# Turning the third pair's second tile behind the first six products of the next tile, with another order of the blocks

## The chip, the cores and the metric

The kernel runs on one core of a Trainium2 chip. The metric is the device time of one execution in microseconds (us), taken as the median of three executions. The core has a matrix engine (PE, with a weight load, PEld, beside it), a vector engine (DVE), a scalar engine (ACT), a general engine (POOL) and a queue for transfers (SP). Each engine takes its instructions in the order in which the program gives them; semaphores hold an instruction back until what it needs is there.

## What is computed

```python
def _A_ref(x, dft_seq_re, dft_seq_im, dft_hid_re, dft_hid_im):
    a = jnp.einsum("bsd,ed->bse", x, dft_hid_re)
    b = jnp.einsum("bsd,ed->bse", x, dft_hid_im)
    return jnp.einsum("ts,bse->bte", dft_seq_re, a) - jnp.einsum("ts,bse->bte", dft_seq_im, b)

def _B_ref(x, w1, b1, w2, b2):
    y = _layernorm(x, axis=-1)
    h = _gelu(jnp.einsum("bsd,df->bsf", y, w1) + b1)
    return jnp.einsum("bsf,fd->bsd", h, w2) + b2

x = A_x
x = x + _A_ref(_layernorm(x, axis=-1), ...)
x = x + _B_ref(_layernorm(x, axis=-1), B_w1, B_b1, B_w2, B_b2)
x = x + _A_ref(_layernorm(x, axis=-1), ...)
x = x + _B_ref(_layernorm(x, axis=-1), B_w1, B_b1, B_w2, B_b2)
```

There are 2048 tokens of 576 values, an inner width of 4608, and two layers of one Fourier mixing and one perceptron each, all in float32. The perceptron's weights are drawn 200 times larger than usual.

## The kernel before

A float32 number is cut into a **high part**, which is the number rounded to a short float format (ACT writes it, in a copy with the output type `F32R`), and a **low part**, which is the rest (DVE subtracts). A product of two numbers then takes three passes on PE: high by high, high by low, low by high (`PASSES`). The large products go by Strassen's scheme with seven block products, numbered 1 to 7, in place of eight. The sums of blocks that this needs are made by DVE and POOL.

A layer is a `Sequence` (the product along the tokens) and then, for each half of 1024 tokens, `hidden` (the product along the 576 values) followed by `mlp` (the perceptron). `hidden` runs four times in the program, and it is what the change touches. It takes eight tiles of 128 tokens, n = 0 to 7. For each it makes 54 products: nine slices k of the inner dimension, three passes, two halves of 288 columns. At the end of a tile DVE adds the result to the tile's x (line 199, shape 128x576), `norms(n)` takes its mean and variance on DVE (L227 to L235), POOL raises the variance to the power -1/2 (L233), and one tile later, ahead of its products, ACT makes the shift (L239) and the normalized tile (L259).

Two tiles that follow each other are a **pair** j. The even tile gives the normalized blocks b11 and b21, the odd one b12 and b22 (each 128 tokens by 288 values; they lie at the places 2, 3 and 0, 1 of `t8[j]`). `mlp` wants them with the tokens along the columns, in seven forms: three of the blocks themselves, and four sums of blocks. For the pairs 0, 1 and 2 this goes as follows.

- `rests(j)`: a block has 288 values, two times 128 and a rest of 32. ACT copies the rests of the four blocks into a small tile `es`, in two groups of 128 columns. In each group one block is the **host**, with three copies of its rest, and another is the **guest**, with one copy in the last 32 columns (L994, L996).
- `turn_blocks(j)`: PE transposes the four blocks (L1010, eight transposes) and the two groups of `es` (L1013, two). ACT copies the result out of PSUM: the eight in one instruction (L1014), then the hosts' rests (L1016) and three copies of the guests' rests (L1020).
- `turn_sums(j)` and `parts`: ACT writes the high parts of the plain blocks (L1028; 128x768 for two blocks, 128x384 for one, 128x1536 for the four sums), DVE their low parts (L202 with a first row of 32 partitions), and DVE makes the four sums of blocks (L202, 128x384, `A<-A`).
- `turn_parts(j)`: the high and low parts of the four sums.

The fourth pair is handled otherwise. Its sums are made by DVE before it is turned (four L202 of 128x288, after a normalization that DVE itself makes on line 978), and `turn_y` transposes seven blocks one after the other (L1059, 14 transposes; its rests on L1069), ACT and DVE cutting them straight from PSUM (`split`, L205 and L202). `mlp` is a generator; its first seven steps are 7 products of 256 columns each, on the first two pairs, and they stand between the last tile's products and `turn_y`: five of them ahead of L1059, the other two behind it.

The order is written out by hand in the loop over n:

```python
            if n in (3, 5):
                turn_parts((n - 3) // 2)
            if n >= 2 and n % 2 == 0:
                turn_blocks(n // 2 - 1)
            if n == NP - 2:
                turn_sums(2)
```

So the pair 2 (the tiles 4 and 5) is turned after the products of tile 6. The normalization of tile 6 stands at the head of the round of tile 7, behind it. The table `RIGHT_T` says at which place of `y` each of the seven forms lies.

Of the kernel before, what the change touches and what calls it, by code (L numbers as in the profile page):

```python
# [10 lines left out]
AF = mybir.ActivationFunctionType  # L11
# [4 lines left out]
P = 128  # L16
NT = S // P
DH = D // 2
NP = NT // 2
# [20 lines left out]

RIGHT = {1: 0, 3: 1, 2: 2, 5: 3, 6: 4, 7: 5, 4: 6}
LEFT = {1: 0, 2: 1, 4: 2, 5: 3, 6: 4, 7: 5, 3: 6}
RIGHT_T = {3: 0, 2: 1, 1: 2, 5: 3, 7: 4, 6: 5, 4: 6}

OUTER = ((1, 6, 5, 3), (7, 4, 2))
LAST = (1, 2, 6, 5, 7, 3, 4)
# [115 lines left out]
def spectral_mixer(ctx: ExitStack, tc: tile.TileContext, x, dh, c0, cs, w1, b1, w2, b2, out):  # L162
# [8 lines left out]
    nc = tc.nc  # L171
# [18 lines left out]
    ident = const.tile([P, P], F32, name="ident")  # L190
# [7 lines left out]
    def add(engine, dst, a, b, op=OP.add):  # L198
        engine.tensor_tensor(dst, a, b, op=op)  # L199

    def sub(engine, dst, a, b):
        engine.tensor_tensor(dst, a, b, op=OP.subtract)  # L202

    def split(hi, lo, src):
        nc.scalar.activation(hi, src, AF.Copy)  # L205
        sub(nc.vector, lo, src, hi.bitcast(F32))
# [4 lines left out]
    def mm(o, a, b, start, stop):  # L211
        nc.tensor.matmul(o, a, b, start=start, stop=stop, skip_group_check=True)  # L212
# [122 lines left out]
    class Sequence:  # L335
# [405 lines left out]
        def post(self, t, i):  # L741
# [26 lines left out]
            if i == 6 and self.late or t == NT - 1 and i == 4:  # L768
# [3 lines left out]
                self.late = None  # L772

        def run(self, hidden):
            for p in range(NP):
                while self.ready <= p:
# [43 lines left out]
    class Hidden:  # L820
# [106 lines left out]
        def turn(self, n, place=None):  # L927
            if n >= NP:
                return
            v = self.uv[n](2 * D)  # L930
            v = (v.bitcast(F32) if self.half else v).rearrange("p (q k t) -> p k q t", q=4, t=32)
            self.ut[n] = place or R.place(UT_AT[self.half][n % 2], 2 * KH * P)
            o = self.ut[n](2, KH, 4, 32)
            split(o[:, 0], o[:, 1], v)
            yield
            self.uvs.give(self.uv.pop(n))

    def drain(*gens):
        gens = list(gens)
        while gens:  # L940
            for g in list(gens):
                if next(g, "end") == "end":
                    gens.remove(g)

    def hidden(h, mlp):
# [4 lines left out]
        def space():  # L950
            return pp[ring.pop(0)] if ring else h.space()
# [6 lines left out]
        y = Y(7, 5, TC)  # L958
# [31 lines left out]
        def rests(j):  # L990
            v = t8[j](8, DH)
            if j < 3:
                e = es(7 * 3 * 32)[:, :2 * P].rearrange("p (n c i) -> p n c i", n=2, c=4)
                nc.scalar.activation(e[:, :, 0:3], v[:, 1:4:2, None, 2 * P:].to_broadcast([P, 2, 3, 32]), AF.Copy)  # L994
                for n, k in enumerate((2, 0)):
                    nc.scalar.activation(e[:, n, 3], v[:, k, 2 * P:], AF.Copy)  # L996
                return
            e = es(7, 3, 32)
            nc.scalar.activation(e[:, :, 1].bitcast(F32R), v[:, 1:8, 2 * P:], AF.Copy)
            nc.gpsimd.tensor_copy(e[:, :, 0], v[:, 1:8, 2 * P:])  # L1000
            sub(nc.gpsimd, e[:, :, 2], v[:, 1:8, 2 * P:], e[:, :, 1])

        def turn_blocks(j):


            v, x = t8[j](8, DH), t8[j](8 * DH)[:, 6 * P:].rearrange("p (b k t) -> p b k t", b=4, k=3)
            a, b = space(), space()
            for n, e in enumerate((2, 0, 1, 3)):
                for k in range(2):
                    nc.tensor.transpose(a[:, n // 2, (n % 2 * 2 + k) * P:(n % 2 * 2 + k + 1) * P],  # L1010
                                        v[:, e, k * P:(k + 1) * P], ident)
            for n in range(2):
                nc.tensor.transpose(b[:, 0, n * P:(n + 1) * P], es(7 * 3 * 32)[:, n * P:(n + 1) * P], ident)  # L1013
            nc.scalar.activation(x[:, :, 0:2], a.rearrange("p a (b k t) -> p (a b) k t", k=2, t=P), AF.Copy)  # L1014
            o = b[:, 0, :2 * P].rearrange("p (b t) -> p b t", t=P)
            nc.scalar.activation(x[:96, 2:4, 2], o[:96], AF.Copy)  # L1016
            if j == 2:
                parts(j, slice(2, 4), slice(0, 2), low=False)
            for c in range(3):
                nc.scalar.activation(x[32 * c:32 * c + 32, 0:2, 2], o[96:], AF.Copy)  # L1020

        def parts(j, block, i, high=True, low=True, engine=nc.vector):


            x = t8[j](8 * DH)[:, 6 * P:].rearrange("p (b k t) -> p b k t", b=4, k=3)[:, block]
            at = slice(j * P, (j + 1) * P)
            if high:
                nc.scalar.activation(y[:, i, 0:3, at], x, AF.Copy)  # L1028
            if low:
                sub(engine, y[64:96, i, 2, at], x[64:96, :, 2], y[64:96, i, 2, at].bitcast(F32))  # L1030
                sub(nc.vector, y[:, i, 3:5, at], x[:, :, 0:2], y[:, i, 0:2, at].bitcast(F32))

        def turn_sums(j):
            x = t8[j](8 * DH)[:, 6 * P:].rearrange("p (b k) -> p b k", b=4)
            b11, b12, b22, b21 = (x[:, k] for k in range(4))
            parts(j, slice(2, 4), slice(0, 2), high=j < 2)
            parts(j, slice(0, 1), slice(2, 3))
            g = nc.vector
            sub(g, b11, b12, b11)
            sub(g, b12, b22, b12)  # L1040
            sub(g, b22, b22, b11)
            sub(g, b21, b21, b22)

        def turn_parts(j):
            parts(j, slice(0, 4), slice(3, 7))
            t8s.give(t8.pop(j))

        def turn_y(j):
            v = t8[j](8, DH)
            at = slice(j * P, (j + 1) * P)  # L1050
            blocks = (1, 3, 2, 4, 5, 6, 7)
            for m, i0 in enumerate((2, 4, 0, 6)):
                if m % 2 == 0:
                    o = space()
                ob = o[:, m % 2]
                ni = min(2, 7 - i0)
                for i in range(ni):
                    for k in range(2):
                        nc.tensor.transpose(ob[:, (2 * i + k) * P:(2 * i + k + 1) * P],  # L1059
                                            v[:, blocks[i0 + i], k * P:(k + 1) * P], ident)  # L1060
                ov = ob[:, :2 * ni * P].rearrange("p (i k t) -> p i k t", k=2, t=P)
                split(y[:, i0:i0 + ni, 0:2, at], y[:, i0:i0 + ni, 3:5, at], ov)
                yield
            o = space()
            for i0 in (0, 4):
                ov = o[:, i0 // 4].rearrange("p (i t) -> p i t", t=P)
                ni = min(4, 7 - i0)
                for i in range(ni):
                    nc.tensor.transpose(ov[:96, i], es(7, 96)[:, blocks[i0 + i] - 1], ident)  # L1069
                nc.scalar.activation(y[:96, i0:i0 + ni, 2, at], ov[:96, :ni], AF.Copy)  # L1070
                yield
            t8s.give(t8.pop(j))

        ln = iter(())
        for n in range(NP):
            h.load(n + 2)
            for k in (n,) if n < NP - 1 else (n, n + 1):
                h.keep_d(k)
            if n:
                drain(turn(n + 1))  # L1080
                next(ln)
            if n >= 2 and n % 2 == 0:
                rests(n // 2 - 1)
            if n == NP - 3:
                next(mlp)
            o = space()
            if n == NP - 1:

                h.uvs.close()
                next(mlp)  # L1090
                o, ring = pp[3], [2, 3] * 3
            u = h.ut.pop(n)
            for k in range(KH):
                if n == 0 and k == KH // 2:
                    drain(turn(1))
                if n in (3, 5) and k == 2:
                    turn_sums((n - 3) // 2)
                if k == 4:
                    next(ln, None)
                for m, (a, b) in enumerate(PASSES):  # L1100
                    for e in range(2):
                        mm(o[:, e, :DH], u(2, KH, P)[:, a, k], h.dd[k][b](2, DH)[:, e],
                           k == 0 and m == 0, k == KH - 1 and m == 2)
            u.free()
            clock[0] += 1
            tile_x = xv[:, :, order[n]]
            add(nc.vector, tile_x, o[:, :, :DH], tile_x)
            ln = norms(n)
            next(ln)
            if n in (3, 5):  # L1110
                turn_parts((n - 3) // 2)
            if n >= 2 and n % 2 == 0:
                turn_blocks(n // 2 - 1)
            if n == NP - 2:
                turn_sums(2)


        for _ in range(2):
# [27 lines left out]
    def mlp(hid, store, first, ends, before, after):  # L1146
# [102 lines left out]
        def inner(q, part=None):  # L1249
# [12 lines left out]
            for i in ORDER:  # L1262
                if part != 0:
                    load_w(2, 1)
                w = got1[q, i](5, P)
                yi = y[:, RIGHT_T[i]][:, :, at]
                o = b[BANK[i]][:, at]
# [267 lines left out]
```

## Time and profile before

| | |
|---|---|
| median of three executions | 2617.44 us |
| the three | 2616.97, 2617.44 and 3634.14 us |
| the profiled execution | 2617.61 us |
| its span, first to last instruction | 2615.8 us |
| PE busy | 2609.1 us of the span, 17228 products and transposes |
| DVE, ACT, POOL busy | 1826.2, 1133.5, 788.8 us |
| granted PE clock | full speed in all 40 slices |

Between the profiled execution's time and its span lie 1.8 us around the first and the last instruction. A row of the timeline has its start, its length, the engine, the line, the operation, what is written and read, the shape, and how many instructions were merged into it; idle time ahead of it and what ended that stand in brackets. Of instructions that overlap, a row's length runs to the end of the last one.

### The profile page before, as it was taken

What the parts mean: (1) busy time and instruction counts of PE and PEld (TensorE: products, weight loads), DVE (VectorE), ACT (ScalarE), POOL (GpSimd) and SP (SyncE); (2) the same over time, 40 slices, a digit from 0 to 9 for tenths busy, and PEclk for the clock granted to TensorE, in tenths of its full rate; (3) what the DMA queues carried; (4) which work ended last, traced back from release to release, by engine and by line L of the source; (5) the groups of instructions that cost most, each with busy time, mean ns of one, the idle gap of its engine ahead of it and who ended that gap; (6) DMA issues with size and microseconds to landing.
All of it is one profiled execution on the core that took longest, in us unless ns stands there. A gap on an engine that the chain in (4) does not pass through costs nothing.

```text
span 2615.8 us, 44812 instructions
## 1 busy us (share of the span) xinstructions
PE 2609.1 (100%) x17228; PEld 2463.2 (94%) x17228; DVE 1826.2 (70%) x2581; ACT 1133.5 (43%) x1881; POOL 788.8 (30%) x639
## 2 busy tenths in 40 slices
PE   9999999999999999999999999999999999999999
PEld 9999999899999989999999999999999999899998
DVE  9999987878777765556687667576555557555555
ACT  7555556555553543333354433353333325433332
POOL 6334333545443332122340000133222232322222
PEclk9999999999999999999999999999999999999999
DMA  6666676778788566666544333756666685666664
GB/s 226 216 248 245 240 252 217 282 273 300 280 288 309 164 209 193 195 220 203 181 178 138 117 121 119 210 166 191 196 196 196 195 268 169 199 195 194 194 195 154
DMA packets 223237, 544.89 MB, mean 208 GB/s; under 512 B 23712, under 2 KB 74912, under 8 KB 222880
## 3 DMA queue, kind: packets, MB, share of 16 engines
q1 hardware_dynamic: 210352, 513.58, 60.9%
q10 hardware_dynamic: 12672, 28.45, 2.8%
q8 instruction: 136, 2.23, 0.3%
q14 instruction: 77, 0.63, 0.1%
HBM read 429.87 MB, written 114.72 MB: 208 GB/s over the span
## 4 chain that ended last, share of the span: by engine, by line
PE 97%; ACT 1%; DVE 1%; issue 0%; DMA 0%; POOL 0%; ACTq 0%; DVEq 0%; POOLq 0%
PE bank L212 96%; PE bank L1010 0%; DVE R L202 0%; PE bank L1461 0%; DMA w_parts<-R 0%; ACT A L259 0%; DVE A L202 0%; PE bank L1059 0%; ACT R L205 0%; ACT A L1020 0%; DVE A L199 0%; POOL moments L233 0%; DVE moments L227 0%; PE bank L1069 0%; ACT R L1028 0%
## 5 line engine op out<-in xcount | busy, mean ns | idle before, releaser
L212 PE MATMUL bank<-R 128*128 128x288 f32 (+2 forms) x16972 | 2582.3, 314 | 0.6 <-ACT A L759 0.2
L212 PEld LDWEIGHTS bank<-R 128*128 128x128 f32 x16972 | 2434.0, 188 | 144.6 <-DVE A L199 1.1
L199 DVE TENSOR_TENSOR A<-bank,A 128x576 f32<-128x576 f32 (+3 forms) x812 | 568.1, 707 | 513.5 <-PE bank L212 457.7
L202 POOL TENSOR_TENSOR R<-A,R 128x512 fp32r<-128x512 f32 (+1 forms) x292 | 379.5, 1308 | 907.7 <-ACT R L1324 565.6
L202 DVE TENSOR_TENSOR R<-A,R 128x1024 fp32r<-128x1024 f32 (+10 forms) x534 | 530.7, 1017 | 56.1 <-ACT R L714 26.0
L1324 ACT ACTIVATE R<-A 128x512 fp32r<-128x512 f32 x288 | 177.4, 630 | 354.8 <-DVE A L202 221.2
L199 POOL TENSOR_TENSOR A<-A 128x576 f32<-128x576 f32 (+2 forms) x102 | 151.4, 1493 | 532.5 <-ACT A L759 359.1
L1259 ACT ACTIVATE bank<-bank,b1t 128x512 f32<-128x512 f32 (+1 forms) x224 | 144.9, 647 | 351.1 <-DVE bank L199 232.6
L199 DVE TENSOR_TENSOR bank<-bank,A 128x512 f32<-128x512 f32 (+1 forms) x228 | 152.3, 670 | 143.3 <-PE bank L212 142.7
L714 ACT ACTIVATE R<-A 128x1024 fp32r<-128x1024 f32 x196 | 204.2, 1053 | 107.0 <-PE bank L212 62.1
L202 POOL TENSOR_TENSOR A<-A 128x288 f32<-128x288 f32 (+3 forms) x152 | 192.1, 1268 | 187.2 <-DVE R L202 112.6
L202 DVE TENSOR_TENSOR A<-A 128x1024 f32<-128x1024 f32 (+3 forms) x166 | 159.0, 962 | 5.3
L202 DVE TENSOR_TENSOR R<-bank,R 128x512 fp32r<-128x512 f32 x232 | 156.2, 676 | 5.5 <-ACT R L1324 5.0
L1324 ACT ACTIVATE R<-bank 128x512 fp32r<-128x512 f32 x216 | 121.4, 595 | 34.4 <-PE bank L212 34.4
L202 DVE TENSOR_TENSOR A<-bank,A 128x512 f32<-128x512 f32 x144 | 98.1, 681 | 0.3
L1286 ACT ACTIVATE A<-bank 128x512 f32<-128x512 f32 (+1 forms) x76 | 43.8, 577 | 114.4 <-PE bank L212 114.3
L285 ACT ACTIVATE R<-A 128x256 fp32r<-128x256 f32 x126 | 51.9, 412 | 85.1 <-DMA w_parts<-R 56.5
L1259 ACT ACTIVATE A<-bank,b1t 128x512 f32<-128x512 f32 (+1 forms) x76 | 50.6, 665 | 63.8 <-DVE bank L199 63.8
L233 POOL TENSOR_TENSOR moments<-moments,power 128x1 f32<-128x1 f32 x32 | 25.6, 799 | 142.8 <-DVE moments L235 114.3
L286 ACT ACTIVATE R<-A,power,middle 128x128 fp32r<-128x128 f32 x126 | 60.6, 481 | 0.0
L259 ACT ACTIVATE A<-A,moments 128x576 f32<-128x576 f32 x58 | 49.3, 867 | 21.6 <-DMA A<-x_mid 11.2
L1194 ACT ACTIVATE R<-A 128x576 fp32r<-128x576 f32 x63 | 42.2, 676 | 16.6 <-DVE A L202 7.1
(74 smaller groups left out, 617.2 us busy)
## 6 DMA issues: line engine op xcount, KB each, us to landing
R<-w_parts SPq DMA_DIRECT2D x504, 320.0 KB, 3.4
R<-w_parts SPq DMA_DIRECT2D x189, 576.0 KB, 3.7
A<-in_cs SPq DMA_DIRECT2D x112, 512.0 KB, 4.5
w_parts<-R SPq DMA_DIRECT2D x63, 576.0 KB, 6.0
w_parts<-R ACTq DMA_DIRECT2D x76, 320.0 KB, 4.9
uv_mid<-A SPq DMA_DIRECT2D x28, 576.0 KB, 5.7
w_parts<-R SPq DMA_DIRECT2D x50, 320.0 KB, 4.8
A<-in_w SPq DMA_DIRECT2D x72, 192.0 KB, 5.4
```

Source lines behind the costliest of these rows:

```text
L199: engine.tensor_tensor(dst, a, b, op=op)
L202: engine.tensor_tensor(dst, a, b, op=OP.subtract)
L212: nc.tensor.matmul(o, a, b, start=start, stop=stop, skip_group_check=True)
L233: nc.gpsimd.tensor_tensor(mv[:, 3:4], mv[:, 2:3], power[:, 0:1], op=OP.pow)
L259: nc.scalar.activation(dst, src, AF.Identity, bias=mv[:, 4:5], scale=mv[:, 3:4])
L285: nc.scalar.activation(t[:, 1:4:2], src[:, 0:3:2], AF.Copy)
L286: nc.scalar.activation(t[:, 2], src[:, 1], AF.Identity, bias=power[:, 2:3], scale=middle)
L714: nc.scalar.activation(self.cells[t, i](2, NP, P)[:, 0], self.source(t, i), AF.Copy)
L1194: nc.scalar.activation(got2[g, i](2, 2, DH)[:, :, 0], src, AF.Copy)
L1259: nc.scalar.activation(dst, src, AF.Gelu_apprx_tanh, bias=bias(f))
L1286: nc.scalar.activation(up, o, AF.Copy)
L1324: nc.scalar.activation(H[q, k](2, TC)[:, 0], src, AF.Copy)
```

## The change

The second tile of the pair 2 is turned apart from the first. `turn_blocks` becomes a generator with a `yield` after the four transposes of the even tile; what is left (the four of the odd tile, the two groups of rests, and all copies) and `turn_sums(2)` run inside tile 7, behind its slice k = 0, which is six products. The hosts of the rests are b22 and b11, where they were b22 and b21, and the guests b12 and b21, where they were b11 and b12; by their places in `t8[j]` the copies of the rests are two instructions, not three. In `turn_sums` three of the four sums stand ahead of the low part of the guest block b21. `RIGHT_T` and the slices in `turn_y` follow the new places in `y`; the order in which `turn_y` transposes its blocks stays.

```diff
-RIGHT_T = {3: 0, 2: 1, 1: 2, 5: 3, 7: 4, 6: 5, 4: 6}
+RIGHT_T = {3: 0, 2: 1, 1: 2, 6: 3, 7: 4, 5: 5, 4: 6}
...
-                nc.scalar.activation(e[:, :, 0:3], v[:, 1:4:2, None, 2 * P:].to_broadcast([P, 2, 3, 32]), AF.Copy)
-                for n, k in enumerate((2, 0)):
-                    nc.scalar.activation(e[:, n, 3], v[:, k, 2 * P:], AF.Copy)
+                nc.scalar.activation(e[:, :, 0:3], v[:, 1:3, None, 2 * P:].to_broadcast([P, 2, 3, 32]), AF.Copy)
+                nc.scalar.activation(e[:, :, 3], v[:, 0:4:3, 2 * P:], AF.Copy)
...
-            for n, e in enumerate((2, 0, 1, 3)):
+            for n, e in ((2, 2), (3, 3), (1, 0), (0, 1)):
+                if n == 1:
+                    yield
...
-            nc.scalar.activation(x[:96, 2:4, 2], o[:96], AF.Copy)
+            nc.scalar.activation(x[:96, 0:3:2, 2], o[:96], AF.Copy)
             if j == 2:
-                parts(j, slice(2, 4), slice(0, 2), low=False)
+                parts(j, slice(0, 3, 2), slice(0, 3, 2), low=False)
             for c in range(3):
-                nc.scalar.activation(x[32 * c:32 * c + 32, 0:2, 2], o[96:], AF.Copy)
+                nc.scalar.activation(x[32 * c:32 * c + 32, 1:4:2, 2], o[96:], AF.Copy)
...
-            b11, b12, b22, b21 = (x[:, k] for k in range(4))
-            parts(j, slice(2, 4), slice(0, 2), high=j < 2)
-            parts(j, slice(0, 1), slice(2, 3))
+            b22, b12, b11, b21 = (x[:, k] for k in range(4))
+            parts(j, slice(0, 3, 2), slice(0, 3, 2), high=j < 2)
             g = nc.vector
             sub(g, b11, b12, b11)
             sub(g, b12, b22, b12)
             sub(g, b22, b22, b11)
+            parts(j, slice(3, 4), slice(1, 2))
             sub(g, b21, b21, b22)
...
-                split(y[:, i0:i0 + ni, 0:2, at], y[:, i0:i0 + ni, 3:5, at], ov)
+                split(y[:, two, 0:2, at], y[:, two, 3:5, at], ov)
...
+                if n == NP - 1 and k == 1:
+                    drain(rest_of_blocks)
+                    turn_sums(2)
...
-            if n >= 2 and n % 2 == 0:
-                turn_blocks(n // 2 - 1)
+            if n in (2, 4):
+                drain(turn_blocks(n // 2 - 1))
             if n == NP - 2:
-                turn_sums(2)
+                rest_of_blocks = turn_blocks(2)
+                next(rest_of_blocks)
```

Lines behind the edits move by up to six: L1010 becomes L1011, L1013 becomes L1014, L1014, L1016, L1020 and L1028 become L1015, L1017, L1021 and L1029, L996 becomes L995, L1059 becomes L1061, L1286 becomes L1292.

On PE, at the end of each `hidden`, these are the rows from the third pair's transposes (`bank<-ident,A`) over the products of tile 7 (`bank<-R`, 128x288) to the first products of `mlp` (128x256) and the transposes of the fourth pair:

```order
-L1010 MATMUL bank<-ident,A 128x128 x8
-L1013 MATMUL bank<-ident,A 128x128 x2
-L212 MATMUL bank<-R 128x288 x54
+L1011 MATMUL bank<-ident,A 128x128 x4
+L212 MATMUL bank<-R 128x288 x6
+L1011 MATMUL bank<-ident,A 128x128 x4
+L1014 MATMUL bank<-ident,A 128x128 x2
+L212 MATMUL bank<-R 128x288 x48
 L212 MATMUL bank<-R 128x256 x35
-L1059 MATMUL bank<-ident,A 128x128 x14
+L1061 MATMUL bank<-ident,A 128x128 x14
```

Four of the ten transposes stay ahead of tile 7; six products now stand ahead of the other six.

On ACT the same place reads as follows before, from the normalization of tile 5 (the first row) to the copy of `mlp`'s first result (the last):

```order
L259 ACTIVATE A<-A,moments 128x576 [waits Activation_49]
L994 ACTIVATE A<-A 128x2x96 [waits Activation_49]
L996 ACTIVATE A<-A 128x32 x2
L1014 ACTIVATE A<-bank 128x4x256 [waits PE_49,Activation_49]
L1016 ACTIVATE A<-bank 96x2x128 [waits PE_49]
L1028 ACTIVATE R<-A 128x2x3x128 [waits Activation_49]
L1020 ACTIVATE A<-bank 32x2x128 x3
L1028 ACTIVATE R<-A 128x3x128 [waits Activation_49]
L239 ACTIVATE moments<-moments,power 128x1 [waits DVE_49,Pool_49]
L259 ACTIVATE A<-A,moments 128x576 [waits Activation_49]
L1286 ACTIVATE A<-bank 128x256 [waits PE_49]
```

And with the change:

```order
L259 ACTIVATE A<-A,moments 128x576 [waits Activation_49]
L994 ACTIVATE A<-A 128x2x96 [waits Activation_49]
L995 ACTIVATE A<-A 128x2x32
L239 ACTIVATE moments<-moments,power 128x1 [waits DVE_49,Pool_49]
L259 ACTIVATE A<-A,moments 128x576 [waits Activation_49]
L1015 ACTIVATE A<-bank 128x4x256 [waits PE_49]
L1017 ACTIVATE A<-bank 96x2x128 [waits PE_49]
L1029 ACTIVATE R<-A 128x2x3x128 [waits Activation_49]
L1021 ACTIVATE A<-bank 32x2x128 x3
L1029 ACTIVATE R<-A 128x3x128 [waits Activation_49]
L1292 ACTIVATE A<-bank 128x256 [waits PE_49]
```

The shift and the normalization of tile 6 (L239 and the second L259), which stood behind all copies and high parts of the pair 2, stand ahead of them now, because they are issued at the head of round 7 and the rest of the turning inside it.

On DVE, the end of `turn_sums` and the addition of the next tile's result (L199), the same in all three pairs:

```order
 L202 TENSOR_TENSOR R<-A,R 32x2x128
 L202 TENSOR_TENSOR R<-A,R 128x2x2x128
+L202 TENSOR_TENSOR A<-A 128x384 x3
 L202 TENSOR_TENSOR R<-A,R 32x128
 L202 TENSOR_TENSOR R<-A,R 128x2x128
-L202 TENSOR_TENSOR A<-A 128x384 x4
+L202 TENSOR_TENSOR A<-A 128x384
 L199 TENSOR_TENSOR A<-bank,A 128x2x288
 L227 BN_STATS moments<-A 128x6 x2
```

Three of the four sums moved ahead of the guest's low part (the rows of 32x128 and 128x2x128); the number of instructions is the same.

More of the change, by code (lines that the diff above doesn't have):

```diff
@@ L1050, in turn_y @@
             at = slice(j * P, (j + 1) * P)
-            blocks = (1, 3, 2, 4, 5, 6, 7)
-            for m, i0 in enumerate((2, 4, 0, 6)):
+            blocks = (1, 3, 2, 6, 5, 4, 7)
+            for m, (two, turned_first) in enumerate(((slice(2, 6, 3), 0), (slice(3, 5), 1),
+                                                     (slice(0, 2), 0), (slice(6, 7), 0))):
                 if m % 2 == 0:
@@ L1055, in turn_y @@
                 ob = o[:, m % 2]
-                ni = min(2, 7 - i0)
-                for i in range(ni):
+                of = blocks[two]
+                for i in sorted(range(len(of)), key=lambda i: i != turned_first):
                     for k in range(2):
                         nc.tensor.transpose(ob[:, (2 * i + k) * P:(2 * i + k + 1) * P],
-                                            v[:, blocks[i0 + i], k * P:(k + 1) * P], ident)
-                ov = ob[:, :2 * ni * P].rearrange("p (i k t) -> p i k t", k=2, t=P)
-                split(y[:, i0:i0 + ni, 0:2, at], y[:, i0:i0 + ni, 3:5, at], ov)
+                                            v[:, of[i], k * P:(k + 1) * P], ident)
+                ov = ob[:, :2 * len(of) * P].rearrange("p (i k t) -> p i k t", k=2, t=P)
+                split(y[:, two, 0:2, at], y[:, two, 3:5, at], ov)
                 yield
```

## The prediction

> **What bounds the kernel now.** I read the page's busy shares and the chain that ended last, then the list of waits on PE, then the timeline of one `hidden` engine by engine.
>
> ```profile
> PE 2609.1 (100%) x17228; PEld 2463.2 (94%) x17228; DVE 1826.2 (70%) x2581; ACT 1133.5 (43%) x1881; POOL 788.8 (30%) x639
> ...
> PE bank L1010 <- ACT A L259: 1.5, 4, 0.4
> PE bank L1461 <- POOL ident masks.py:199: 1.3, 1, 1.3
> PE bank L212 <- ACT A L759: 0.2, 1, 0.2
> ```
>
> PE has work all the time, so another engine's time counts only where it makes PE wait. PE's waits sum to some 3 us in 2615.8; half of that, 1.5 us, stands four times, once in each `hidden`, at the third pair's transposes. No wait at all is listed at L1059, the fourth pair's transposes. Of the first `hidden`, PE:
>
> ```profile
> 424.99 0.38 PE L1010 MATMUL bank<-ident,A 128*128 128x128 f32 x2
> 425.74 0.87 PE L1010 MATMUL bank<-ident,A 128*128 128x128 f32 x6 [0.36 <-ACT A L259]
> 426.45 0.38 PE L1013 MATMUL bank<-ident,A 128*128 128x128 f32 x2
> 426.58 11.63 PE L212 MATMUL bank<-R 128*128 128x288 f32 x89
> 438.05 1.80 PE L1059 MATMUL bank<-ident,A 128*128 128x128 f32 x14
> 439.60 1.92 PE L212 MATMUL bank<-R 128*128 128x256 f32 x14
> ```
>
> Two transposes run, then PE waits 0.36 us for the normalization of tile 5. From 425.74 to 426.45 six transposes start, so one takes about 0.11 us; the 54 products of tile 7 and 35 of `mlp` fill 426.58 to 438.05, 0.13 us each. ACT and POOL beside it:
>
> ```profile
> 424.81 0.87 ACT L259 ACTIVATE A<-A,moments 128x576 f32<-128x576 f32 x1
> 425.71 0.36 ACT L994 ACTIVATE A<-A 128x192 f32<-128x192 f32 x1
> 425.99 0.33 ACT L996 ACTIVATE A<-A 128x32 f32<-128x32 f32 x2
> 426.71 1.03 ACT L1014 ACTIVATE A<-bank 128x1024 f32<-128x1024 f32 x1 [0.39 <-PE bank L1010]
> 427.63 0.37 ACT L1016 ACTIVATE A<-bank 96x256 f32<-96x256 f32 x1
> 428.03 0.85 ACT L1028 ACTIVATE R<-A 128x768 fp32r<-128x768 f32 x1
> 428.90 1.16 ACT L1020 ACTIVATE A<-bank 32x256 f32<-32x256 f32 x3
> 430.10 0.52 ACT L1028 ACTIVATE R<-A 128x384 fp32r<-128x384 f32 x1
> 430.53 0.37 ACT L239 ACTIVATE moments<-moments,power 128x1 f32<-128x1 f32 x1
> 430.94 0.87 ACT L259 ACTIVATE A<-A,moments 128x576 f32<-128x576 f32 x1
> 434.88 0.39 ACT L1286 ACTIVATE A<-bank 128x256 f32<-128x256 f32 x1 [3.07 <-PE bank L212]
> ...
> 428.62 0.55 POOL L233 TENSOR_TENSOR moments<-moments,power 128x1 f32<-128x1 f32 x1 [0.88 <-DVE moments L235]
> ```
>
> And DVE, which takes up tile 6 at 426.38 and tile 7 at 434.04:
>
> ```profile
> 418.81 2.34 DVE L202 TENSOR_TENSOR A<-A 128x384 f32<-128x384 f32 x4
> 421.07 0.75 DVE L199 TENSOR_TENSOR A<-bank,A 128x576 f32<-128x576 f32 x1
> ...
> 423.26 3.19 DVE L202 TENSOR_TENSOR R<-A,R 32x512 fp32r<-32x512 f32 x3
> 426.38 0.75 DVE L199 TENSOR_TENSOR A<-bank,A 128x576 f32<-128x576 f32 x1
> ...
> 428.91 1.12 DVE L202 TENSOR_TENSOR R<-A,R 32x256 fp32r<-32x256 f32 x2 [0.37 <-ACT R L1028]
> 430.65 0.72 DVE L202 TENSOR_TENSOR R<-A,R 32x128 fp32r<-32x128 f32 x2 [0.62 <-ACT R L1028]
> 431.48 2.34 DVE L202 TENSOR_TENSOR A<-A 128x384 f32<-128x384 f32 x4
> 434.04 0.76 DVE L199 TENSOR_TENSOR A<-bank,A 128x576 f32<-128x576 f32 x1 [0.22 <-PE bank L212]
> 436.89 0.58 DVE L978 TENSOR_SCALAR A<-A,moments 128x576 f32<-128x576 f32 x1 [0.38 <-POOL moments L233]
> 437.50 1.69 DVE L202 TENSOR_TENSOR A<-A 128x288 f32<-128x288 f32 x4
> ```
>
> The reader is to see the last row beside PE's L1059 at 438.05. The four sums of the fourth pair end one by one from 437.95 to 439.19, some 0.4 us apart, and PE turns the two halves of tile 6's block and then these sums in that order. The third to end (t2, at about 438.7) is the one that PE reaches as its seventh transpose, 438.05 + 6 x 0.11 = 438.7. **There is no slack.** What delays DVE between 434.04 and 437.5 delays PE by the same.
>
> **The change part by part.** *PE's order.* Four transposes of tile 4 run without waiting, from 424.99 to about 425.43; the 0.36 us goes. Four of the six products follow, to about 425.97. The fifth needs the low part of tile 7's operand, the last of the three instructions in DVE's row at 423.26, which ends at 426.45. So PE waits about 0.5 us there instead, then makes two products, six transposes and 48 products. The end of tile 7: before 426.58 + 54 products; now 426.5 + 2 products + 6 x 0.11 + 48 products, with 4 products or 0.53 us less but 0.66 us of transposes more: 426.63 in place of 426.58. The wait that is removed is thus replaced by one of the same size: **0.0 us** (bounds 0.36 us gained, 0.2 us lost, per `hidden`).
>
> *ACT's order.* This is where the cost lies. The shift of tile 6 (L239) waits for POOL's power, which ends at 428.62 + 0.55 = 429.17. Before, the copies and high parts of the pair ran in that time; now all of them are queued behind the waiting L239. By the starts above one after the other: L239 429.2, L259 429.6, L1015 430.53 (+0.9), L1017 431.45 (+0.92), L1029 of two blocks 431.85 (+0.40), which ends at 432.70 instead of 428.88. The guests' copies end at 433.9, the second L1029 at 434.45. The copy of `mlp`'s first result, due at 434.88, is still on time.
>
> *DVE's order.* DVE's first low part waits for that L1029 and starts at 432.73 in place of 428.91, 3.8 us later; it takes 1.12 us, to 433.85. Then come a 0.10 us changeover (430.65 + 0.72 = 431.37 against 431.48), three sums at 2.34 / 4 = 0.59 us (to 435.73), the guest's low part 0.72 (436.45), a second changeover 0.10 and the last sum 0.56: 437.1. Only behind it stands the addition of tile 7: about 437.05 in place of 434.04. **3.0 us later.** The two waits of 0.37 and 0.62 us and the 0.22 us ahead of 434.04 were DVE's cover, and they are counted in this.
>
> *The same reorder in the first two pairs.* One more changeover, 0.1 us, in the pair ahead moves 421.07 and with it 426.38, POOL's power and all of the above by 0.05 to 0.1 us. I take 0.05. (Bounds: nothing, if the changeover appears only once; 0.1.) The Trainium skill (VectorE: DVE Perf Modes, Terms) says that the pipeline is emptied after every operation, so an order of the same instructions would cost the same: then the 0.15 us go, and the sum is 0.6 us lower. The rows speak against that: the addition of tile 5 starts at 421.07, ahead of the end of the sums before it at 418.81 + 2.34 = 421.15.
>
> *Behind that.* With DVE 3.05 us later, the fourth pair's sums end from 441.0 to 442.2. PE comes to L1061 at 438.1, turns the two halves that are ready, and waits from about 438.3 to 441.05; the later transposes wait for some 0.1 to 0.2 us more. Everything that follows (ACT's table load, `split`, the rest of `mlp`'s steps) is shifted with PE, since DVE and PE keep their distance. PE has no idle time later in which this could be made up.
>
> *The rest.* One activation fewer per pair (L996 twice 0.33 us, so about 0.12 us): in the first two pairs ACT then waits for PE at L1014 anyway, in the third for POOL; nothing. The places in `y` change addresses and make two slices strided; no row shows one strided and one not, and the nearest is that L1028 goes by its elements (128x768 0.85 us, 128x384 0.52 us): nothing, with bounds of 0.1 us either way on each of `split`'s four, beside PE's 14 products at 439.60. No transfer and no instruction of the SP or POOL queue moves; the low part of the sums on POOL comes 2 us later, ahead of transposes that come 3 us later.
>
> *Sum.* Four `hidden` of 3.05 us: 12.2 us. The profiled execution took 2617.61 us, which gives 2629.8; the median shown is 0.17 us lower, so **2629.6 us**, 0.5% more. The bounds of the terms (2.7 to 3.3 us each) give 2628.2 to 2630.6.
>
> **Rivals.** *Not slower: the late copies are hidden* (2616.1 to 2617.6 us). The mechanism is the one named in the change: PE's only regular wait goes, 4 x 0.36 us, and nothing replaces it, or just the wait for tile 7's low part. It decides if DVE reaches the addition of tile 7 by 434.04, that is if its lows of the third pair need not wait for L239: if DVE took them after tile 7, or ACT the copies ahead of the shift. For it: the wait of 0.36 us is real, and PE needs only tile 7's own products in this time. Against: the engines take their rows in order, and the shift's wait for POOL shows in the program's own order. 10%.
>
> *Slower still: PE's clock falls in the new wait* (about 2639 us). The start of the trace shows PE at half pace (a row of the chain, then two stretches with PE's busy time and instructions first):
>
> ```profile
> 1.35 8.17 PE bank L1461 x52
> ...
> 3.00:6.00 3.00, 3.00 (x16) 3.00 (x15) 2.41 (x9) 0.00 (x0) 0.61 (x2) 1.00 0.96 287
> 6.00:9.00 3.00, 3.00 (x29) 3.00 (x28) 2.56 (x7) 2.50 (x5) 0.76 (x1) 1.00 1.03 376
> ```
>
> The same transposes come 16 in 3 us and then 29 in 3 us, and the column of the granted clock (1.00) does not tell the two apart. From PE's start at 1.35 us to about 6 us half of 4.6 us is lost, 2.3 us. If a wait of 2.8 us puts PE back into that state, each `hidden` loses up to 2.3 us more, 9.2 us in all. The trace has no wait above 1.3 us in which to see it. 5%. The Trainium skill (TensorE: Matmul & The Clock Gate, Why this matters for your kernels) sets the limit at idle gaps of about 3 us; by that rule my 2.8 us would just pass. Its window of 3.4 us at half rate would cost an estimated 1.7 us each, 2636 us.
>
> **How the numbers follow.** The forecast has 82%, the hidden copies 10%, the clock 5%; 3% is left for something I don't see. The forecast's own range is 2628.2 to 2630.6 by its terms; executions of the same program differ by 0.6 us here (2616.97 to 2617.61) and chips may add as much again, so 2626 to 2633, which holds the 82%. Faster by over 2% would take 52 us out of 3 us of waits: 0.5%. Slower by over 2% needs 13 us in each `hidden`: 1%. Within 2%, which is about what a measurement of this kernel can tell from no change: 98.5%.
>
> **What would show it.** In the profile after, the list of PE's waits has no L1011 on ACT L259; it has L212 on DVE L202 four times about 0.5 us, and L1061 on DVE L202 with a longest of 2.5 to 3 us. ACT is idle ahead of the third pair's L239 for some 2.8 us with POOL as the releaser. DVE's addition of tile 7 stands 3 us behind the end of tile 7's products. I am wrong if L1061 waits for nothing, or if L239 stands behind L1015 in the trace, or if L1061's products run at a pitch of 0.2 us after the wait.

## The result, and the profile after

The changed kernel takes **2634.93 us** (median of six executions, 2632.80 to 2635.99) against 2618.02 us for the kernel before: ratio **1.0064**, interval 1.0050 to 1.0078. (One execution of the kernel before took 3634 us; the ratio leaves it out, and without it the median is 2617.97 us.) It is slower by 17 us where 12 were forecast, and lies 2 us above the stated range.

The profiled execution took 2635.07 us. The head of its page, and the list of PE's waits (line, what it waited for, us in total, times, longest):

```profile
span 2633.3 us, 44801 instructions
PE 2615.9 (99%) x17228; PEld 2469.5 (94%) x17228; DVE 1825.7 (69%) x2581; ACT 1134.6 (43%) x1869; POOL 789.0 (30%) x639
...
PE bank L1061 <- DVE A L202: 9.9, 4, 2.5
PE bank L212 <- DVE R L202: 2.3, 5, 0.8
PE bank L1467 <- POOL ident masks.py:199: 1.4, 1, 1.4
```

The wait of the third pair's transposes for ACT L259 is gone. In its place PE waits four times 2.47 us at the fourth pair's transposes, and L212 waits for a low part, 0.3 to 0.4 us in each `hidden` and 0.8 us once elsewhere. These waits sum to 12.2 us, which is 10.7 more than the 1.5 us of before. But the span grew by 17.5 us, so waits alone don't explain it: PE's busy time rose too, from 2609.1 to 2615.9 us, for the same 17228 instructions.

The first `hidden`, on PE:

```profile
424.58 0.60 PE L1011 MATMUL bank<-ident,A 128*128 128x128 f32 x4
424.94 0.77 PE L212 MATMUL bank<-R 128*128 128x288 f32 x4
426.12 0.54 PE L212 MATMUL bank<-R 128*128 128x288 f32 x2 [0.41 <-DVE R L202]
426.50 0.60 PE L1011 MATMUL bank<-ident,A 128*128 128x128 f32 x4
...
437.74 0.38 PE L1061 MATMUL bank<-ident,A 128*128 128x128 f32 x2
440.60 2.77 PE L1061 MATMUL bank<-ident,A 128*128 128x128 f32 x12 [2.47 <-DVE A L202]
443.02 2.40 PE L212 MATMUL bank<-R 128*128 128x256 f32 x14
445.26 0.93 PE L1071 MATMUL bank<-ident,A 128*96 128x128 f32 x7
```

On ACT and on DVE:

```profile
425.60 0.24 ACT L995 ACTIVATE A<-A 128x64 f32<-128x64 f32 x1
428.82 0.39 ACT L239 ACTIVATE moments<-moments,power 128x1 f32<-128x1 f32 x1 [2.98 <-POOL moments L233]
429.24 0.87 ACT L259 ACTIVATE A<-A,moments 128x576 f32<-128x576 f32 x1
430.13 1.03 ACT L1015 ACTIVATE A<-bank 128x1024 f32<-128x1024 f32 x1
431.06 0.37 ACT L1017 ACTIVATE A<-bank 96x256 f32<-96x256 f32 x1
431.46 0.85 ACT L1029 ACTIVATE R<-A 128x768 fp32r<-128x768 f32 x1
```

```profile
425.99 0.75 DVE L199 TENSOR_TENSOR A<-bank,A 128x576 f32<-128x576 f32 x1
...
432.34 1.12 DVE L202 TENSOR_TENSOR R<-A,R 32x256 fp32r<-32x256 f32 x2 [4.19 <-ACT R L1029]
433.57 1.82 DVE L202 TENSOR_TENSOR A<-A 128x384 f32<-128x384 f32 x3
435.40 0.72 DVE L202 TENSOR_TENSOR R<-A,R 32x128 fp32r<-32x128 f32 x2
436.15 0.56 DVE L202 TENSOR_TENSOR A<-A 128x384 f32<-128x384 f32 x1
436.63 0.75 DVE L199 TENSOR_TENSOR A<-bank,A 128x576 f32<-128x576 f32 x1
```

The reader is to see one chain: ACT idle for 2.98 us ahead of the shift of tile 6, DVE idle for 4.19 us behind it, tile 7's addition at 436.63. From tile 6's addition to tile 7's DVE takes 10.64 us; before it took 7.66 (426.38 to 434.04).

What is left shows in PE's clock. Stretches of one `hidden` of the changed kernel (start and end, length, busy time and instructions of PE, PEld, DVE, ACT and POOL, then the granted clock, the DMA share and GB/s):

```profile
437.28:440.70 3.42, 0.95 (x9) 0.71 (x8) 2.83 (x9) 2.69 (x3) 0.55 (x1) 1.00 0.00 0
440.70:444.11 3.41, 3.41 (x17) 3.22 (x18) 3.20 (x8) 2.31 (x6) 2.03 (x3) 0.50 0.01 1
```

Behind the wait the clock is at **half for 3.41 us**, in each of the four `hidden` of this execution. In the first `hidden`, 12 transposes took 2.77 us (1.80 us for 14 before), the next 14 products 2.40 us (1.92 before). The six executions had a mean granted clock of 0.997 (three, this one among them), 0.998 (one) and 0.999 (two), so not every execution had all four falls.

So theory A: the order on ACT delays DVE, DVE delays PE by 2.47 us, and that wait costs a second time, through the clock. The experiments take these apart. In all of them "before" is the kernel before on the same chip, 2618.1 to 2618.5 us.

### The profile page after: what moved, and what is told of

Same layout as the page of the kernel before. It is cut to its first block, busy times and chain, and to the rows that moved or that the text cites. A ratio compares the mean times of both kernels' runs of the same rounds, so it can differ in the third digit from the quotient of the medians.

```text
span 2633.3 us, 44801 instructions
## 1 busy us (share of the span) xinstructions
PE 2615.9 (99%) x17228; PEld 2469.5 (94%) x17228; DVE 1825.7 (69%) x2581; ACT 1134.6 (43%) x1869; POOL 789.0 (30%) x639
## 4 chain that ended last, share of the span: by engine, by line
PE 63%; DVE 1%; ACT 0%; issue 0%; DMA 0%; POOL 0%; DVEq 0%; ACTq 0%; POOLq 0%
PE bank L212 62%; DVE R L202 0%; PE bank L1061 0%; DVE A L202 0%; DVE A L199 0%; DVE moments L227 0%; PE bank L1011 0%; DMA R<-w_parts 0%; ACT A L259 0%; ACT R L1029 0%; PE bank L1071 0%; ACT A L1021 0%; DVE A L978 0%; POOL moments L233 0%; ACT A L1015 0%
## 5 line engine op out<-in xcount | busy, mean ns | idle before, releaser
L212 PE MATMUL bank<-R 128*128 128x288 f32 (+2 forms) x16972 | 2586.1, 314 | 2.8 <-DVE R L202 2.3
L212 PEld LDWEIGHTS bank<-R 128*128 128x128 f32 x16972 | 2436.9, 189 | 147.1 <-DVE R L202 2.6
L199 DVE TENSOR_TENSOR A<-bank,A 128x576 f32<-128x576 f32 (+3 forms) x812 | 567.9, 707 | 519.5 <-PE bank L212 460.5
L199 POOL TENSOR_TENSOR A<-A 128x576 f32<-128x576 f32 (+2 forms) x102 | 151.5, 1494 | 529.9 <-ACT A L759 355.8
L199 DVE TENSOR_TENSOR bank<-bank,A 128x512 f32<-128x512 f32 (+1 forms) x228 | 152.4, 670 | 144.8 <-PE bank L212 144.0
L1292 ACT ACTIVATE A<-bank 128x512 f32<-128x512 f32 (+1 forms) x76 | 43.8, 577 | 104.9 <-PE bank L212 103.2
L259 ACT ACTIVATE A<-A,moments 128x576 f32<-128x576 f32 x58 | 49.3, 867 | 21.6 <-DMA A<-x_mid 11.3
L1029 ACT ACTIVATE R<-A 128x768 fp32r<-128x768 f32 (+2 forms) x36 | 33.3, 946 | 44.0 <-DVE A L202 43.8
```

The costliest lines, as they stand in the source:

```text
L259: nc.scalar.activation(dst, src, AF.Identity, bias=mv[:, 4:5], scale=mv[:, 3:4])
L1292: nc.scalar.activation(up, o, AF.Copy)
```

## The experiments

**The order on ACT put back, the split kept.**

```diff
             if n:
                 drain(turn(n + 1))
-                next(ln)
+                if n < NP - 1:
+                    next(ln)
...
                 if n == NP - 1 and k == 1:
                     drain(rest_of_blocks)
+                    next(ln)
                     turn_sums(2)
```

> The change as it is, but the shift and the normalization of tile 6 (L239, L259) are issued behind the rest of the third pair's turning instead of ahead of it; PE's order and DVE's order stay. Theory A (the order on ACT holds DVE's lows back, DVE reaches tile 7 some 2.6 us late, PE waits 2.47 us at the fourth pair's transposes, and that wait lowers its clock for 3.4 us): L1061 waits for less than 0.3 us, no record of half clock in the span, the wait of 0.4 us for tile 7's low part stays; 2617.5 to 2620 us. Rival B (the split on PE itself, six products between the transposes, is what costs): nothing changes, 2633 to 2636 us.

Measured: 2619.73 us, ratio 1.0004 (0.9995 to 1.0014). ACT, DVE and PE of the first `hidden`:

```profile
429.71 1.16 ACT L1021 ACTIVATE A<-bank 32x256 f32<-32x256 f32 x3
430.89 0.39 ACT L239 ACTIVATE moments<-moments,power 128x1 f32<-128x1 f32 x1
...
434.05 0.76 DVE L199 TENSOR_TENSOR A<-bank,A 128x576 f32<-128x576 f32 x1
...
426.45 0.53 PE L212 MATMUL bank<-R 128*128 128x288 f32 x2 [0.73 <-DVE R L202]
438.05 1.81 PE L1061 MATMUL bank<-ident,A 128*128 128x128 f32 x14
```

With the shift behind the copies, DVE adds tile 7 at 434.05, L1061 runs without a wait, and no `hidden` has a record of half clock. The 17 us are gone although the split on PE is still there. Rival B has fallen. What the split leaves is the wait for tile 7's low part (0.73 us here, 0.4 in the other three).

**The order on ACT alone, in the kernel before.**

```diff
             if n:
                 drain(turn(n + 1))
-                next(ln)
+                if n < NP - 1:
+                    next(ln)
...
+            if n == NP - 2:
+                next(ln)
             if n >= 2 and n % 2 == 0:
                 turn_blocks(n // 2 - 1)
```

> The kernel before with one thing moved: the shift and the normalization of tile 6 ahead of the third pair's turning; PE's rows, hosts and sums are those of before. Theory A: this alone brings the loss back. ACT's chain ends as in the change, and DVE now has the guest's low part ahead of all four sums, so tile 7's addition is some 3.5 us late, PE waits about 3 us at L1059 four times (12 to 14 us) and its clock falls four times (3.4 us at half, 1.7 us each): 2636 to 2640 us. Rival B: no loss without the split, 2617 to 2619 us.

Measured: 2637.61 us, ratio 1.0071 (1.0056 to 1.0086).

```profile
428.93 0.39 ACT L239 ACTIVATE moments<-moments,power 128x1 f32<-128x1 f32 x1 [2.89 <-POOL moments L233]
...
437.77 0.38 PE L1059 MATMUL bank<-ident,A 128*128 128x128 f32 x2
441.22 2.82 PE L1059 MATMUL bank<-ident,A 128*128 128x128 f32 x12 [3.06 <-DVE A L202]
```

Without any split the same chain appears, with a wait of 3.06 us. It is longer than 2.47 because the guest's low part still stands ahead of all sums, and DVE waits 0.62 us for ACT's second high part there. Together the two runs show that the order on ACT is both needed and enough for the loss.

**Work for PE in the wait: a run that came out otherwise.** The first attempt at filling the wait had its condition behind the loop instead of in it, so that no filler was ever issued and the program was the change itself.

```diff
                         nc.tensor.transpose(ob[:, (2 * i + k) * P:(2 * i + k + 1) * P],
                                             v[:, of[i], k * P:(k + 1) * P], ident)
+                if m == 0 and i == 0:
+                    for _ in range(18):
+                        nc.tensor.transpose(o[:, 1, :P], ident, ident)
```

> The change with 18 transposes of the identity into a free part of PSUM, standing on PE behind the first two of L1061, where PE waits; they fill about 1.96 of the 2.47 us and change no result. Theory A, where any work on PE keeps the clock: no record of half clock in the span, the wait shrinks to about 0.5 us, the time falls by the clock's share alone (4 x 1.7 us) to 2627 to 2629.5 us. Rival D (transposes do not count as work for the clock, or the clock falls for another reason): half clock is still recorded four times and the time stays at 2634 to 2638 us.

Measured: 2635.71 us, ratio 1.0063 (1.0048 to 1.0078), the change once more. Neither theory is tested by it, but its trace is of use: the wait of 2.47 us is there four times, and the clock fell only in the last two `hidden`. Those two took 30.7 us each, counted from the third pair's first transpose to the 70th instruction of PE behind the first L1074, and the first two 29.3: the same program with the same wait, and 1.4 us between them. (The span is 2635.1 us all the same, 1.8 us more than in the profile after: PE waits elsewhere in this trace, 1.5 us for ACT L757 and 1.2 us for a transfer among others.) The first `hidden`:

```profile
444.03 1.83 PE L1061 MATMUL bank<-ident,A 128*128 128x128 f32 x12 [2.47 <-DVE A L202]
...
439.42:442.84 3.42, 2.14 (x18) 1.90 (x17) 2.90 (x8) 2.64 (x2) 0.52 (x1) 1.00 0.03 7
442.84:446.25 3.41, 2.22 (x17) 1.90 (x18) 3.10 (x8) 1.60 (x5) 0.84 (x3) 1.00 0.00 0
```

The same wait, and the same 12 transposes in 1.83 us, not 2.77. The stretches quoted are parts of a grid: in every trace that has them the records of half clock begin on points that are whole multiples of 3.413 us apart (in the changed kernel's 139.0, 245.0 and 139.0 of them), and inside the program they end on such points. Here a point of the grid fell into the middle of the wait, and PE was idle for 37% of one part and 35% of the next. In the profile after, the part ahead of the fall was idle for 72% (0.95 of 3.42 us busy).

**The other order of blocks alone, without the split.**

```diff
-                if n == NP - 1 and k == 1:
-                    drain(rest_of_blocks)
-                    turn_sums(2)
...
-            if n in (2, 4):
+            if n >= 2 and n % 2 == 0:
                 drain(turn_blocks(n // 2 - 1))
             if n == NP - 2:
-                rest_of_blocks = turn_blocks(2)
-                next(rest_of_blocks)
+                turn_sums(2)
```

> The change without the split: the third pair is turned whole behind tile 6, as before; what stays is the other order of blocks, the two rest copies in place of three, three sums ahead of the guest's low part, and the strided places in y. Theory A: these cost nothing that PE sees; the wait of 0.36 us in each hidden is back; 2617 to 2619.5 us. Rival C (the order of blocks or the strided slices have a share in the 17 us): 2621 us or more.

Measured: 2618.47 us, ratio 1.0000 (0.9991 to 1.0010). Rival C has fallen: the new hosts, the three sums ahead of the low part and the strided slices together cost nothing that this comparison can tell, which is some 2.5 us, and PE's rows show no new wait in `hidden`. The wait at the third pair's transposes, which I expected back at 0.36 us, is 0.10 to 0.15 us, since four transposes of the even tile now stand ahead of the odd tile's.

**The wait filled with 18 transposes, with 9, and with 17 products.** The filler's condition now stands inside the loop, behind the first two transposes of L1061:

```diff
                     for k in range(2):
                         nc.tensor.transpose(ob[:, (2 * i + k) * P:(2 * i + k + 1) * P],
                                             v[:, of[i], k * P:(k + 1) * P], ident)
+                    if m == 0 and i == 0:
+                        for _ in range(18):
+                            nc.tensor.transpose(o[:, 1, :P], ident, ident)
```

> The change with 18 transposes of the identity into a free part of PSUM, now really on PE behind the first two of L1061 (in the run before, their condition was never true). They start where PE waits and fill 18 x 0.11 = 1.96 of the 2.47 us; no result changes. Theory A with work of any kind keeping the clock: no half clock in the span, a wait of about 0.5 us is left at L1061, the time is that of the wait alone, 2627 to 2630 us. Rival D (transposes don't count as work for the clock): the stretches of 3.41 us without a product are still followed by half clock, and the time stays at 2633 to 2638 us.

```diff
-                        for _ in range(18):
+                        for _ in range(9):
```

> The same with 9 transposes, so that about 1.49 us of PE's wait are left. In the traces so far the clock fell at the end of a grid of 3.413 us, and only behind those parts of the grid with an idle share of 0.54 or more (0.47 at most where it did not fall). 1.49 us is at most 0.44 of such a part. If the idle share decides: no half clock, the same 2627 to 2630 us as with 18. If any wait well over 1 us may do it: half clock in some hidden, 1.7 us for each.

```diff
-                            nc.tensor.transpose(o[:, 1, :P], ident, ident)
+                            mm(o[:, 1, :2 * P], y[:, 2, 0, :P], y[:, 2, 0, :2 * P], True, True)
```

(17 of these.)

> The same place filled with 17 products of 256 columns on operands that are there (into the same free part of PSUM), 2.0 us; no result changes. Theory A: no half clock, 2627 to 2630 us, as with 18 transposes. Rival D: this one alone keeps the clock, the one with 18 transposes doesn't.

Measured: 2632.14, 2630.99 and 2630.04 us; ratios 1.0053 (1.0037 to 1.0068), 1.0048 (1.0035 to 1.0062) and 1.0045 (1.0032 to 1.0059). None of the three has a record of half clock in its span, and the mean granted clock was 1.000 in all twelve of their executions. With 18 transposes (L1065 is the filler), then with 9:

```profile
438.70 2.13 PE L1065 MATMUL bank<-ident 128*128 128x128 f32 x18
441.33 1.83 PE L1061 MATMUL bank<-ident,A 128*128 128x128 f32 x12 [0.51 <-DVE A L202]
```

```profile
438.32 1.15 PE L1065 MATMUL bank<-ident 128*128 128x128 f32 x9
440.96 1.83 PE L1061 MATMUL bank<-ident,A 128*128 128x128 f32 x12 [1.49 <-DVE A L202]
442.54 1.92 PE L212 MATMUL bank<-R 128*128 128x256 f32 x14
444.30 0.93 PE L1074 MATMUL bank<-ident,A 128*96 128x128 f32 x7
```

PE comes to L1061 and leaves it as in the change, only at full clock: 12 transposes in 1.83 us. Nine were enough here; the idle share of a part of the grid is then at most 44%. Rival D has fallen for this place: with 9, a part of the grid that held no product, only transposes, kept the clock (the row has the columns of the stretches above):

```profile
438.84:442.25 3.41, 1.92 (x15) 1.35 (x14) 2.93 (x9) 1.59 (x3) 0.55 (x1) 1.00 0.00 0
442.25:445.66 3.41, 3.41 (x32) 3.41 (x30) 3.23 (x5) 3.11 (x8) 3.14 (x4) 1.00 0.30 79
```

All three medians lie above the expected 2627 to 2630 us, by 0.04 to 2.1 us, though their intervals reach into it. By the times alone the clock's part can't be told, since the three intervals overlap with that of the change (1.0050 to 1.0078); it rests on the traces and the granted clock. The traces put the waits' part, with 9, at 11.7 us over the four `hidden`.

**A version without either wait.** The split behind the first four products, which don't need tile 7's low part, and the order on ACT put back:

```diff
                 for m, (a, b) in enumerate(PASSES):
+                    if n == NP - 1 and k == 0 and m == 2:
+                        drain(rest_of_blocks)
+                        next(ln)
+                        turn_sums(2)
                     for e in range(2):
```

> A version with both waits avoided: the split stands behind the first four products of tile 7 (those that don't need the low part), and the shift and normalization of tile 6 are issued behind the rest of the turning. Theory A: no wait at the third pair's transposes, at tile 7's fifth product or at L1061 above 0.15 us, 4 x 0.36 us less than before, ratio 0.9994 (2617 us against 2618.5), which the interval will hardly tell from no change. Rival: DVE still comes 0.5 us late to tile 7 and the gain is given back at L1061, ratio 1.000 or more.

Measured: 2616.89 us (2615.96 to 2618.36), ratio 0.9995 (0.9986 to 1.0004).

```profile
425.70 0.60 PE L1011 MATMUL bank<-ident,A 128*128 128x128 f32 x4
426.06 0.78 PE L212 MATMUL bank<-R 128*128 128x288 f32 x4
426.68 0.60 PE L1011 MATMUL bank<-ident,A 128*128 128x128 f32 x4
427.11 0.38 PE L1014 MATMUL bank<-ident,A 128*128 128x128 f32 x2
427.25 11.11 PE L212 MATMUL bank<-R 128*128 128x288 f32 x85
438.19 1.81 PE L1061 MATMUL bank<-ident,A 128*128 128x128 f32 x14
```

No row of PE in `hidden` waits any more, and DVE is not late: its addition of tile 7 waits 0.25 us for PE. From the third pair's first transpose to L1061 PE takes 12.49 us (425.70 to 438.19), before 13.06 (424.99 to 438.05). Its median is the lowest of all the kernels here, but the interval takes in no change: a gain of 1 or 2 us is less than such a comparison can tell.

## Why the prediction was wrong, point by point

Over the four `hidden`, from the third pair's first transpose to the 70th instruction of PE behind L1071's first, PE took 105.6 us before, 122.2 us with the change and 117.3 us with the change and 9 transposes in the wait. So of the 17.5 us between the two spans 11.7 are the wait and its neighbours, 4.9 the clock, and 0.9 lies elsewhere, where the 0.8 us wait is.

- *The wait removed is replaced by one of the same size* (expected 0.5 us at the fifth product): right, 0.41 us.
- *ACT's order*: right in its mechanism and its numbers. L239 waits for POOL, the first L1029 comes right behind L1015 and L1017, and DVE starts on the third pair's lows 6.35 us behind tile 6's addition (425.99 to 432.34), which I had at 432.73 against 426.38, the same 6.35.
- *DVE 3.0 us later, 3.05 with the first pairs' share*: measured 2.98 (10.64 against 7.66). The second changeover of 0.10 us does not appear; the last sum starts 0.03 us behind the low part (435.40 + 0.72 to 436.15). That was the lower bound of this term. Tile 7's addition still starts ahead of the last sum's end (436.63 against 436.71), so the emptying after every operation that the Trainium skill states (VectorE: DVE Perf Modes, Terms) isn't what these two records show.
- *PE waits from about 438.3 to 441.05*: measured 438.1 to 440.60, a wait of 2.47 us where 2.75 were expected. The sum of 12.2 us was close to what the waits alone cost, 11.7 us.
- *The rest costs nothing*: right within some 2.5 us, by the run with the blocks' order alone.
- **The step that failed is the rival on PE's clock**, which I put at 5% and left out of the sum and the range. It came in addition to the forecast's wait, in all four `hidden` of the profiled execution, and cost 4.9 us where the sum had nothing. The sign that I had named for it is there: 12 transposes of L1061 start in 2.42 us (440.60 to 443.02), a pitch of 0.20 us. My argument against it was that the trace showed no wait long enough, which is no evidence, and that the wait stayed just below a limit that no row of the trace showed. The Trainium skill (TensorE: Matmul & The Clock Gate, Why this matters for your kernels) warns of idle gaps of about 3 us; here 2.47 us was enough, and 2.47 us was also harmless where the grid fell well. The measurement decides. The fall's price was nearer to the estimate of 1.7 us than to my 2.3 us from the program's start: half of 3.41 us is 1.7, of which 1.2 us (4.9 / 4) arrive at the end. Part of the slow stretch lies where PE would have waited for the later sums anyway: at full clock the 12 transposes took 1.83 us, where eleven pitches of 0.11 and a last one of 0.27 make 1.5.
- *DVE and PE keep their distance behind it*: nearly. The one wait of 0.8 us for a low part, 50 us behind the first `hidden` of the profiled execution, wasn't foreseen; that it follows from the change wasn't tried, since waits of this size at other places come and go between runs of the kernels here.

## What to carry to other kernels

When a step is split and its tail issued later, look at what the program now issues ahead of that tail on each of the other engines: here the tail's copies on ACT fell behind one small instruction that waits for another engine, and a removed wait of 0.36 us became one of 2.47 us two engines further on. A forecast for the matrix engine needs the price of a wait twice, its length and what the clock does behind it, and a wait that is longer than any in the trace at hand is to be counted with the second price as a full case. Where a wait can't be avoided, transposes that change no result can be put into it: here nine of them, 1.15 us, kept the clock.

## What the runs showed of the hardware

- The granted clock of PE is decided at the points of a grid of 3.413 us that runs free of the program: in two executions of the same program such points lie at 440.70 and at 442.84 us, 2.14 us apart, which is no multiple of 3.413. In the traces of the change, of its repetition and of the order on ACT alone, it fell to half behind every part in which PE was idle for 54% or more (ten such parts at full clock in the `hidden`, 54% to 81%), and behind none with 47% or less, the runs with fillers included. Between these two shares stands one part, at the program's end in the version without either wait: PE was idle for 52% of it (1.64 of 3.41 us busy), and the clock stayed. That the share decides, and not another property of the wait, was inferred: in each of these parts the idle time is one unbroken gap, so its length inside the part sorts them just as well, and the fillers shortened both.
- So the same wait of 2.47 us costs over a microsecond more or not, by where it falls on the grid: the fall came four times of four in one trace of the same program and twice of four in another, there with 1.4 us between a `hidden` with it and one without.
- It stayed at half for one part of the grid in nine of the ten falls, with PE idle for 9% of that part at most. In the kernel with the order on ACT alone, one fall lasted two parts, 6.83 us: PE was idle for 30% of the first of them (2.39 of 3.41 us busy).

```profile
915.36:918.77 3.41, 2.39 (x11) 2.29 (x12) 3.16 (x8) 1.18 (x3) 0.99 (x2) 0.50 0.01 2
918.77:922.19 3.42, 3.42 (x18) 3.42 (x17) 3.42 (x6) 1.28 (x4) 3.28 (x2) 0.50 0.01 2
922.19:925.60 3.41, 3.41 (x30) 3.40 (x29) 1.03 (x3) 1.75 (x5) 1.66 (x2) 1.00 0.21 37
```

- Transposes alone count as work for the clock: with 9 fillers, a part of the grid without any product was busy for 1.92 of 3.41 us and kept the clock.
